# Attention and feed-forward on one core: load order of the first keys and queries, warm-up products, and the order of the first scores and weighted values

## Chip, cores, metric

One core of a Trainium2 chip. The metric is device time in microseconds (us) of one execution, the median over several runs of the same program. Traces give times from the start of their own span; a span is some 1.7 us shorter than the time of the run (236.55 us of 238.26 before).

## The reference, cut to what matters

```python
# q, k, v: (4, 8, 768, 64); sort_net: (4, 8, 8, 8); out: (3072, 512)
P = sort_net                       # 8 blocks of 96 rows in each head
for _ in range(5):                 # Sinkhorn: exp, then rows and columns normalized
    ...
k_sorted = einsum('bhij,bhjcd->bhicd', P, k_blocks)      # blocks mixed with P
v_sorted = einsum('bhij,bhjcd->bhicd', P, v_blocks)
attn = softmax(q_block @ k_sorted_block.T / 8)           # inside each block of 96
x = attn @ v_sorted_block
h = relu(x @ w_in)                                       # feed-forward, 512 -> 2048 -> 512
out = (s * h * h + b) @ w_out
```

## The kernel before: the parts that matter here

The work is cut into eight tiles of tokens. What concerns us is the head of the program, until the first feed-forward product (tile `hps`) of the first tile of tokens; from there on TensorE is nearly always busy (198.7 of the 201.3 us from 30.73 to 232 us). In the head, q, k and v of batch 0 are loaded (float32 in memory, bfloat16 on chip); q is transposed on TensorE; the Sinkhorn loop runs on VectorE (DVE) and ScalarE (ACT); a small product `pe` spreads its result over the partitions; from that a mixing matrix `pd1` is built; products with it sort the keys (`tk`, cast into `ks`) and the values (`tv`, cast into `vs`); then come scores (`sc`), exp (`at`), weighted values (`pv`, normalized into `x`), and transposes of `x`.

```python
psa = ... tile_pool(name="psa", bufs=3, PSUM)     # large PSUM tiles
psb = ... tile_pool(name="psb", bufs=2, PSUM)     # small ones

nc.sync.dma_start(out=s_bc, in_=moe_s.to_broadcast([128, 1]))   # one scalar to 128 partitions
nc.sync.dma_start(out=b_bc, in_=moe_b.to_broadcast([128, 1]))
...
load_q(0, slice(0, 64));  load_k(*brows(0));  load_v(*brows(0));  load_q(0, slice(64, 128))
...
def warm_up(n):                       # products of zeros that nobody reads, meant to keep the clock up
    for _ in range(n):
        wp = psb.tile([128, 256], FP, tag="b", name="wp")
        nc.tensor.matmul(out=wp, lhsT=zt[:, 0:128], rhs=zt, start=True, stop=True)

def v_piece0(d0, n, eng):             # n of the 64 columns of the sorted v
    ps = (psa if n > 8 else psb).tile([128, n, 64], FP)          # written shorter here
    for t in range(n):
        nc.tensor.matmul(out=ps[:, t, :], lhsT=vb[0:64, :, d0 + t], rhs=pd1[0:64]...)
    evac(VS[0][:, :, d0:d0 + n], ps..., eng)
...
warm_up(38)
q_half(0, "s")                        # 48 transposes of q's first half, two copies on ACT
warm_up(12)
build_pd1()                           # the product pe, then three small steps on DVE
k_piece(...) x 4                      # 48 products, 16 casts on DVE and ACT
v_piece0(0, 16, "v"); v_piece0(16, 16, "s"); v_piece0(32, 16, "v")
s_piece(0, 0); s_piece(0, 1)
v_piece0(48, 16, "v")
s_piece(0, 2); s_piece(0, 3)
q_half(1, "s")
for hp in range(NHP):
    p_piece(0, hp, 0, 2)
t_piece(0, "v", 0, 2)
s_piece(1, 0); s_piece(1, 1)
ffn1(0, ...)                          # the first feed-forward products
```

In the trace before, TensorE took q's transposes (8.34 us), the twelve warm-ups (9.21) and the product `pe` (12.46) in the order of the program: what stands ahead of `build_pd1` on TensorE also runs ahead of it.

The softmax here doesn't subtract the row's maximum and nothing guards it: scores larger than these inputs give would overflow.

Of the kernel before, what the change touches and what calls it, by code (L numbers as in the profile page):

```python
# [9 lines left out]
FP = mybir.dt.float32  # L10
# [8 lines left out]
def kernel(  # L19
# [18 lines left out]
    NHP = H // 2  # L38
# [28 lines left out]
    psb = ctx.enter_context(tc.tile_pool(name="psb", bufs=2, space=bass.MemoryType.PSUM))  # L67
# [10 lines left out]
    def load_q(b, part=slice(0, 128)):  # L78


        if b == B - 1:
            qr[b] = qrp.tile([128, TQ, H, D], BF, tag="qr", name=f"qr{b}")
            for t in range(TQ):
                nc.gpsimd.dma_start(
                    out=qr[b][:, t],
                    in_=q[b][:, t * 128:(t + 1) * 128, :].rearrange("h p d -> p h d"))
            return
        if b not in qr:
            qr[b] = qrp.tile([128, H, TQ, D], BF, tag="qr", name=f"qr{b}")
        nc.gpsimd.dma_start(  # L90
            out=qr[b][part].rearrange("p h t d -> p h (t d)"),
            in_=q[b].rearrange("h (p t) d -> p h (t d)", t=TQ)[part])

    def load_k(rows, prow, n=1):
        for c0 in range(0, BLK, BLK // n):
            cs = slice(c0, c0 + BLK // n)
            nc.gpsimd.dma_start(out=kb[prow, cs, :], in_=kraw[rows, cs, :])

    def load_v(rows, prow):
        nc.gpsimd.dma_start(out=vb[prow, 0:BLK, :], in_=vraw[rows])  # L100

    def brows(b):
        return slice(b * 64, (b + 1) * 64), slice((b % 2) * 64, (b % 2) * 64 + 64)
# [17 lines left out]
    new_vs(1)  # L121
    nc.scalar.activation(out=warm, in_=warm, func=AF.Exp)

    load_q(0, slice(0, 64))
    load_k(*brows(0))
    load_v(*brows(0))
    load_q(0, slice(64, 128))

# [47 lines left out]
    ks = const.tile([128, 64, BLK], BF)  # L176

    def warm_up(n):
        for _ in range(n):
            wp = psb.tile([128, 256], FP, tag="b", name="wp")  # L180
            nc.tensor.matmul(out=wp, lhsT=zt[:, 0:128], rhs=zt, start=True, stop=True)  # L181

    def zero_pad(r0):
# [9 lines left out]
    between = [lambda: zero_pad(BLK), lambda: zero_pad(BLK + 16), lambda: None,  # L193
               lambda: None, lambda: None]
# [45 lines left out]

    QT = {}

    def q_half(half, eng):

        if half == 0:
            QT[0] = qtp.tile([128, NHP, S], BF, tag="qt", name="qt0")
        pr = slice(half * 64, half * 64 + 64)
        ps = psa.tile([128, 2, 1024], BF, tag="a", name="tq")
        for hp in range(NHP):
            for t in range(TQ):  # L250
                c0 = (hp % 2) * TG + t * 64
                for e in range(2):
                    nc.tensor.transpose(out=ps[e * 64:(e + 1) * 64, hp // 2, c0:c0 + 64],  # L253
                                        in_=qr[0][pr, 2 * hp + e, t, :], identity=ident[pr, pr])
        for a in range(2):
            evac(QT[0][:, 2 * a:2 * a + 2, half * TG:(half + 1) * TG].rearrange(
                     "q b (p t) -> q b p t", t=TQ),
                 ps[:, a, 0:2 * TG].rearrange("q (b t p) -> q b p t", b=2, t=TQ), eng)
# [22 lines left out]
    def k_piece(b, c0, nc2, nb, eng):  # L281




        pr = brows(b)[1] if nb == 1 else slice(0, 128)
        rhs = (pd1[pr] if b < 2 else pd2[pr, b - 2]).rearrange("p e m i -> p (e m i)")
        if nc2 * nb > 8:
            ps = psa.tile([128, nc2, nb * 64], FP, tag="a", name="tk")
        else:  # L290
            ps = psb.tile([128, nc2, nb * 64], FP, tag="b", name="tk")
        for c in range(nc2):
            nc.tensor.matmul(out=ps[:, c, :],  # L293
                             lhsT=kb[pr, c0 + 2 * c:c0 + 2 * c + 2, :].rearrange("p c d -> p (c d)"),
                             rhs=rhs, start=True, stop=True)
        g0 = (b % 2) * 32

        def half(cp):
            if b == 0:
                cs = slice(c0 + cp, c0 + 2 * nc2, 2)  # L300
            else:
                cs = slice(cp * (BLK // 2) + c0 // 2, cp * (BLK // 2) + c0 // 2 + nc2)
            for e in range(2):
                evac(ks[e * 64:(e + 1) * 64, g0:g0 + nb * 32, cs].rearrange(
                         "p (b g) c -> p b g c", b=nb),
                     ps[cp * 64:(cp + 1) * 64].rearrange(
                         "p c (b e g) -> p e b g c", b=nb, e=2)[:, e], eng)

        half(0)
        return lambda: half(1)  # L310

    def v_piece0(d0, n, eng):

        if n > 8:
            ps = psa.tile([128, n, 64], FP, tag="a", name="tv")
        else:
            ps = psb.tile([128, n, 64], FP, tag="b", name="tv")
        for t in range(n):
            nc.tensor.matmul(out=ps[:, t, :], lhsT=vb[0:64, :, d0 + t],  # L319
                             rhs=pd1[0:64].rearrange("p e m i -> p (e m i)"),  # L320
                             start=True, stop=True)
        evac(VS[0][:, :, d0:d0 + n], ps[0:BLK].rearrange("p t g -> p g t"), eng)
# [42 lines left out]
    def s_piece(t, hp):  # L365

        b, half = divmod(t, 2)
        g0 = (b % 2) * 32 + hp * NB + half * HB
        sc = psa.tile([BLK, 2, 512], FP, tag="a", name="sc")
        for n in range(HB):  # L370
            for e in range(2):
                pr = slice(e * 64, (e + 1) * 64)
                q0 = (half * HB + n) * BLK
                nc.tensor.matmul(out=sc[:, e, n * BLK:(n + 1) * BLK], lhsT=ks[pr, g0 + n, :],  # L374
                                 rhs=QT[b][pr, hp, q0:q0 + BLK], start=True, stop=True)
        at = atp.tile([BLK, 2, TG], BF, tag="at", name="at")
        nc.scalar.activation(out=at, in_=sc[:, :, 0:TG], func=AF.Exp, scale=scale)  # L377
        AT[t, hp] = at

    def p_piece(t, hp, n0=0, nn=HB):  # L380

        b, half = divmod(t, 2)
        at = AT[t, hp]
        if t not in X:
            X[t] = xp.tile([BLK, HB, d_model], BF, tag="x", name="x")
        x = X[t]
        atf = at.rearrange("p e t -> p (e t)")
        if nn < HB:
            p1 = psb.tile([128, 512], FP, tag="b", name="pv")
            pv = [p1[:, e * nn * VW:(e + 1) * nn * VW] for e in range(2)]  # L390
            pvv = p1[0:BLK, 0:2 * nn * VW].rearrange("p (e n w) -> p e n w", e=2, w=VW)
        else:
            p2 = psa.tile([128, 2, 512], FP, tag="a", name="pv")
            pv = [p2[:, 0], p2[:, 1]]
            pvv = p2[0:BLK, :, 0:nn * VW].rearrange("p e (n w) -> p e n w", w=VW)
        for e in range(2):
            for n in range(n0, n0 + nn):
                c0 = (e * HB + n) * BLK
                m = 128 if c0 + 128 <= 2 * TG else BLK
                gi = e * 32 + hp * NB + half * HB + n  # L400
                nc.tensor.matmul(out=pv[e][0:m, (n - n0) * VW:(n - n0 + 1) * VW],  # L401
                                 lhsT=atf[:, c0:c0 + m],
                                 rhs=VS[b][:, gi, :], start=True, stop=True)
        rec = rtp.tile([BLK, 2, HB], FP, tag="rec", name="rec")
        nc.vector.reciprocal(out=rec[:, :, 0:nn], in_=pvv[:, :, :, D])  # L405
        nc.vector.tensor_tensor(  # L406
            out=x[:, n0:n0 + nn, hp * 128:(hp + 1) * 128].rearrange("p n (e d) -> p e n d", e=2),
            in0=pvv[:, :, :, 0:D],
            in1=rec[:, :, 0:nn].unsqueeze(3).broadcast_to([BLK, 2, nn, D]), op=ALU.mult)
# [141 lines left out]
    def build_pd1():  # L551
        pt = block_rows(0)
        nc.vector.tensor_tensor(  # L553
            out=pd1, in0=hmask.rearrange("p (m e) i -> p e m i", e=2),
            in1=bass.AP(tensor=pt.tensor, offset=pt.offset,
                        ap=[list(pt.ap[0]), [0, 2], [0, NHP], list(pt.ap[1])]),
            op=ALU.mult)
# [10 lines left out]


    warm_up(38)  # L570
    q_half(0, "s")
    warm_up(12)
    build_pd1()
    k_piece(0, 0, 16, 1, "v")()
    k_piece(0, 32, 16, 1, "s")()
    k_piece(0, 64, 8, 1, "v")()
# [2 lines left out]
    v_piece0(16, 16, "s")  # L579
    v_piece0(32, 16, "v")  # L580
    s_piece(0, 0)
    s_piece(0, 1)
    v_piece0(48, 16, "v")
    s_piece(0, 2)
    s_piece(0, 3)
    q_half(1, "s")
    for hp in range(NHP):
        p_piece(0, hp, 0, 2)
    t_piece(0, "v", 0, 2)
    s_piece(1, 0)  # L590
    s_piece(1, 1)
# [105 lines left out]
```

## Time and profile before

| | before |
|---|---|
| median of runs | 239.0 us (238.2 to 239.3) |
| PE / DVE / ACT busy | 95 / 55 / 46 % of the span |
| product `pe` starts | 12.46 us |
| v products can start (v landed) | 16.65 us |
| sorted keys complete | 19.73 us |
| sorted v complete | 25.30 us |
| first feed-forward product | 30.73 us |
| from there to the end of the span | 205.8 us |
| full clock, by the trace's clock records | 5.25 to 15.49 us, and from 32.56 us |

The first two rows are from the runs and the page, the rest from the timeline and the table of stretches. Busy time alone misleads here: in the head, PE is "busy" with warm-ups and with half-speed work. The prediction shows the lines.

### The profile page before, as it was taken

The page shows a single profiled execution, that of the slowest core. Times are in us where ns is not written, and L with a number is a line of the kernel's source. Part 1 is how long each engine was busy: PE and PEld are TensorE (multiplying, and loading weights), DVE is VectorE, ACT ScalarE, POOL GpSimd, SP SyncE. Part 2 cuts the span into 40 slices and gives each one's busy share as a digit, 9 for nine tenths or more (in the row PEclk, how much of TensorE's full clock was granted, in tenths as well). Part 3 has the DMA queues.
Part 4 walks back from the last instruction along what each step waited for, and adds up shares of the span by engine and source line. Part 5 has one row for each costly group of instructions (what it writes and reads, how often), then busy time and mean ns, then how long its engine had stood idle before and what let it go on. Part 6 is the DMA issues. An engine that isn't in the chain of part 4 may idle for free.

```text
span 236.6 us, 4840 instructions
## 1 busy us (share of the span) xinstructions
PE 223.9 (95%) x2029; PEld 134.3 (57%) x2048; DVE 129.8 (55%) x264; ACT 108.8 (46%) x157; POOL 43.7 (18%) x57
## 2 busy tenths in 40 slices
PE   8849799989999999999999999999999999999994
PEld 4548698845545555555555455656554556654443
DVE  4776557967994458866434744434352544342221
ACT  5357556435538542477775321566422225660000
POOL 7820000099960000295000000000000000000000
PEclk9985579999999999999999999999999999999999
DMA  4999999996999996499992414630024142001122
GB/s 57 192 198 212 225 192 206 218 221 121 146 156 175 257 320 124 111 100 109 122 74 90 111 47 115 87 89 1 3 87 105 56 116 42 0 0 44 59 77 89
DMA packets 38231, 28.11 MB, mean 119 GB/s; under 512 B 26433, under 2 KB 32577, under 8 KB 37697
## 3 DMA queue, kind: packets, MB, share of 16 engines
q0 software_dynamic: 13600, 15.21, 45.6%
q1 hardware_dynamic: 24464, 12.53, 22.9%
q8 instruction: 16, 0.26, 0.5%
q10 hardware_dynamic: 144, 0.07, 0.1%
q14 instruction: 7, 0.05, 0.1%
HBM read 29.63 MB, written 8.65 MB: 162 GB/s over the span
## 4 chain that ended last, share of the span: by engine, by line
PE 85%; DMA 6%; DVE 5%; issue 2%; POOL 1%; ACT 1%; POOLq 0%
PE hps L458 35%; PE ops L501 33%; DMA vb<-in_v_dram 6%; PE sc L374 3%; PE pv L401 3%; PE tv L319 2%; PE tk L293 2%; PE ops L486 1%; DVE x L406 1%; PE tq L268 1%; PE tv L349 1%; DVE gt L463 1%; DVE ks L237 1%; DVE vn L237 1%; PE tq L253 1%
## 5 line engine op out<-in xcount | busy, mean ns | idle before, releaser
L458 PE MATMUL hps<-xt,wi 128*128 128x384 bf16 (+1 forms) x576 | 88.7, 310 | 1.0 <-DVE xt L237 1.0
L501 PE MATMUL ops<-wo,gt 128*128 128x512 bf16 x349 | 84.0, 379 | 1.4 <-issue 0.5
L462 ACT ACTIVATE rt<-hps 128x768 bf16<-128x768 f32 (+1 forms) x72 | 53.3, 740 | 51.6 <-PE hps L458 50.5
L458 PEld LDWEIGHTS <-wi 128*128 128x128 bf16 x576 | 53.8, 99 | 31.1 <-issue 2.3
L463 DVE TENSOR_TENSOR gt<-rt 128x768 bf16<-128x768 bf16 (+1 forms) x72 | 42.0, 585 | 41.2 <-ACT rt L462 40.6
L501 PEld LDWEIGHTS <-gt 128*128 128x128 bf16 x368 | 33.6, 98 | 36.8 <-issue 0.6
L475 DVE SCALAR_TENSOR_TENSOR ot<-ops,s_bc,bias 128x512 f32<-128x512 f32 x23 | 17.2, 749 | 40.4 <-PE ops L501 40.3
L377 ACT ACTIVATE at<-sc 96x768 bf16<-96x768 f32 x32 | 24.2, 802 | 33.1 <-PE sc L374 33.1
L406 DVE TENSOR_TENSOR x<-pv,rec 96x512 bf16<-96x512 f32 (+1 forms) x36 | 22.6, 628 | 1.3
L239 ACT CAST ks<-tk 64x512 bf16<-64x512 f32 (+1 forms) x32 | 16.0, 501 | 7.7 <-PE tk L293 7.4
L237 DVE CAST ks<-tk 64x512 bf16<-64x512 f32 (+1 forms) x32 | 18.1, 565 | 1.3 <-PE tk L293 0.9
L622 POOL TENSOR_TENSOR csum<-csum,wo 128x512 f32<-128x512 f32 x14 | 17.6, 1256 | 1.0
L401 PEld LDWEIGHTS <-at 96*128 96x128 bf16 (+1 forms) x256 | 11.9, 104 | 4.1 <-ACT qt L239 1.0
L401 PE MATMUL pv<-vs,at 96*128 96x66 bf16 (+1 forms) x256 | 12.9, 199 | 0.8 <-DVE rec L405 0.6
L405 DVE RECIPROCAL rec<-pv 96x8 f32<-96x8 f32 (+1 forms) x36 | 6.9, 192 | 8.9 <-PE pv L401 8.8
L374 PEld LDWEIGHTS <-ks 64*96 64x96 bf16 x256 | 8.3, 132 | 5.7 <-issue 5.4
L374 PE MATMUL sc<-qt,ks 64*96 64x96 bf16 x256 | 10.7, 223 | 0.0
L181 PE MATMUL wp<-zt 128*128 128x256 bf16 x50 | 9.3, 310 | 1.1 <-DVE warm L113 1.1
L293 PEld LDWEIGHTS <-kb 64*128 64x128 bf16 x192 | 6.4, 95 | 5.4 <-issue 4.9
L293 PE MATMUL tk<-pd,kb 64*128 64x64 bf16 x192 | 7.8, 191 | 0.9 <-DVE pd L553 0.9
L239 ACT CAST vn<-tv 128x1024 bf16<-128x1024 f32 x6 | 6.1, 1012 | 4.1 <-PE tv L349 2.2
L319 PE MATMUL tv<-pd,vb 64*128 64x64 bf16 x64 | 6.0, 271 | 2.0 <-DMA vb<-in_v_dram 1.5
(71 smaller groups left out, 106.6 us busy)
## 6 DMA issues: line engine op xcount, KB each, us to landing
out_dram<-ot SPq DMA_DIRECT2D x23, 256.0 KB, 2.2
kb<-in_k_dram POOLq DMA_DIRECT2D x4, 768.0 KB, 10.4
vb<-in_v_dram POOLq DMA_DIRECT2D x4, 768.0 KB, 19.0
wi<-in_moe_w_in_dram POOLq DMA_DIRECT2D x2, 1024.0 KB, 19.1
wo<-in_moe_w_out_dram POOLq DMA_DIRECT2D x2, 1024.0 KB, 30.3
qr<-in_q_dram POOLq DMA_DIRECT2D x2, 768.0 KB, 27.7
dv<-vn SPq DMA_DIRECT2D x6, 256.0 KB, 7.0
vs<-dv POOLq DMA_DIRECT2D x4, 384.0 KB, 11.9
```

The lines of the kernel that those rows point to most:

```text
L237: nc.vector.tensor_copy(out=out, in_=in_)
L239: nc.scalar.copy(out=out, in_=in_)
L293: nc.tensor.matmul(out=ps[:, c, :], lhsT=kb[pr, c0 + 2 * c:c0 + 2 * c + 2, :].rearrange("p c d -> p (c d)"), rhs=rhs, start=True, stop=True)
L374: nc.tensor.matmul(out=sc[:, e, n * BLK:(n + 1) * BLK], lhsT=ks[pr, g0 + n, :], rhs=QT[b][pr, hp, q0:q0 + BLK], start=True, stop=True)
L377: nc.scalar.activation(out=at, in_=sc[:, :, 0:TG], func=AF.Exp, scale=scale)
L401: nc.tensor.matmul(out=pv[e][0:m, (n - n0) * VW:(n - n0 + 1) * VW], lhsT=atf[:, c0:c0 + m], rhs=VS[b][:, gi, :], start=True, stop=True)
L406: nc.vector.tensor_tensor(out=x[:, n0:n0 + nn, hp * 128:(hp + 1) * 128].rearrange("p n (e d) -> p e n d", e=2), in0=pvv[:, :, :, 0:D], in1 ...
L458: nc.tensor.matmul(out=hps[:, f, 0:nt], lhsT=wi_at(hp, f0 + f), rhs=xt_at(t, hp, n0, nn), start=(hp == 0), stop=(hp == NHP - 1))
L462: nc.scalar.activation(out=rt[:, :, 0:nt], in_=hps[:, :, 0:nt], func=AF.Relu)
L463: nc.vector.tensor_tensor(out=gt[:, f0:f0 + 2, c0:c0 + nt], in0=rt[:, :, 0:nt], in1=rt[:, :, 0:nt], op=ALU.mult)
L501: nc.tensor.matmul(out=ops, lhsT=gt[:, f, m * 128:(m + 1) * 128], rhs=wo_at(f), start=(f == 0), stop=(f == NF - 1))
L622: nc.gpsimd.tensor_tensor(out=csum, in0=csum, in1=wo_at(f), op=ALU.add)
```

## The change

Its intent: start the keys' large load first; let warm-ups run without waits between their two buffers and fill more of the wait for `pd1`, so that TensorE's clock stays up; take the last v product off the wait for the first exp by splitting it and putting its halves between scores; and use the wait of the weighted values for q's second half.

```diff
+    load_k(*brows(0))
     load_q(0, slice(0, 64))
-    load_k(*brows(0))
     load_v(*brows(0))
...
     def warm_up(n):
+        wp = psb.tile([128, 256], FP, tag="b", name="wp")
         for _ in range(n):
-            wp = psb.tile([128, 256], FP, tag="b", name="wp")
             nc.tensor.matmul(out=wp, lhsT=zt[:, 0:128], rhs=zt, start=True, stop=True)
...
-    def q_half(half, eng):
+    def q_half(half, eng, between=lambda hp: None):
...
         for hp in range(NHP):
+            between(hp)
             for t in range(TQ):
...
     warm_up(38)
     q_half(0, "s")
-    warm_up(12)
+    warm_up(20)
     build_pd1()
+    warm_up(6)
...
     s_piece(0, 0)
+    v_piece0(48, 8, "v")
     s_piece(0, 1)
-    v_piece0(48, 16, "v")
+    v_piece0(56, 8, "v")
     s_piece(0, 2)
     s_piece(0, 3)
-    q_half(1, "s")
-    for hp in range(NHP):
-        p_piece(0, hp, 0, 2)
+    q_half(1, "s", lambda hp: p_piece(0, hp, 0, 2))
```

## The prediction

Passages that gave rules or figures of the hardware that no trace of this case shows are cut, and the cuts marked. With them go the end of the 38 warm-ups ahead of q and, as a term of the sum, the time of the twenty behind it. That term, added to q's landing at 10.3 us and 0.94 us of transposes, came to 13.4 us for the start of the spreading product `pe`, "about 1 us" after the 12.46 of the kernel before. This 1.0, the other delays (2.2, 3.3, none) under **Cost** and **Sum**, and the 12.4 us of rival A hold that term, and so does the total: a gain of 1.5 us, from 239.0 to 237.5. "Warm" and "cold" mean full and half granted clock. That a dense stretch of work would hold the clock was the author's estimate, from the drop at 15.49 us after 1.96 us of work in 3.42.

> **What bounds the kernel now.** I read the page first: PE is busy 95% of 236.6 us, and the chain that ended last is 85% PE. Its part by line tells where this change can act.
>
> ```profile
> PE 85%; DMA 6%; DVE 5%; issue 2%; POOL 1%; ACT 1%; POOLq 0%
> ```
>
> The 6% DMA is one wait, for v of batch 0, and it lies before 17 us; from the first feed-forward product on, the chain is almost wholly PE. So what the head of the program (0 to 30.7 us) saves moves everything after it, and nothing after it is changed. Next I read the chain in order of time for 0 to 45 us: the head's skeleton.
>
> ```profile
> 2.67 13.99 DMA vb<-in_v_dram
> 16.65 0.14 issue
> 16.79 4.37 PE tv L319 x47
> ...
> 22.49 1.38 PE tv L319 x14
> ...
> 24.08 1.23 DVE vs L237
> ...
> 25.36 1.49 PE tq L253 x48
> ```
>
> V lands at 16.65, then v products, scores, a fourth v product that starts at 22.49 behind the first exp, its eviction until 25.3, the second half of q (25.36), and only then weighted values. Then the table by stretch of each engine's busy time and granted clock; after the clock column stand DMA share and GB/s:
>
> ```profile
> 8.66:12.07 3.41, 2.57 (x52) 1.58 (x45) 2.76 (x13) 1.74 (x4) 2.55 (x5) 1.00 0.96 198
> 12.07:15.49 3.42, 1.96 (x50) 1.82 (x50) 1.93 (x6) 0.74 (x2) 0.88 (x1) 1.00 1.01 195
> 15.49:18.90 3.41, 2.11 (x24) 2.14 (x25) 3.29 (x7) 3.33 (x7) 0.54 (x1) 0.50 1.18 210
> ...
> 29.14:32.56 3.42, 3.42 (x39) 3.01 (x40) 0.98 (x2) 1.84 (x3) 0.00 (x0) 0.50 1.07 185
> 32.56:35.97 3.41, 3.41 (x53) 3.06 (x51) 2.96 (x12) 1.85 (x5) 0.00 (x0) 1.00 1.24 207
> ```
>
> From 15.49 to 32.56 us, 17 us, TensorE ran at half clock. Last I read the timeline of the head:
>
> ```profile
> 9.21 2.02 PE L181 MATMUL wp<-zt 128*128 128x256 bf16 x12
> 12.46 0.40 PE L222 MATMUL pe<-sn,emat 32*128 32x64 f32 x2 [1.23 <-DVE sn L210]
> 13.77 1.56 PE L293 MATMUL tk<-pd,kb 64*128 64x64 bf16 x48 [0.90 <-DVE pd L553]
> 14.43 4.90 DVE L237 CAST ks<-tk 64x512 bf16<-64x512 f32 x8 [0.71 <-PE tk L293]
> 14.89 4.83 ACT L239 CAST ks<-tk 64x512 bf16<-64x512 f32 x8 [2.68 <-PE tk L293]
> 19.36 1.22 DVE L237 CAST vs<-tv 96x1024 bf16<-96x1024 f32 x1
> 30.73 1.46 PE L458 MATMUL hps<-xt,wi 128*128 128x192 bf16 x8
> ```
>
> A second limit shows here: the sorted keys' casts keep DVE and ACT full from 14.4 to 19.7, whatever the clock of TensorE. They start as soon as the mixing matrix pd is there (13.7).
>
> [...] the low stretch is 17.07 us, five windows of 3.41, and the drop follows a window (12.07 to 15.49) with only 1.96 us of PE, most of it on half the rows. [...] Warm-ups until 5.20 us took 4.06 us for 19 or 214 ns each, [...] the twelve later ones 2.02/12 = 168 ns[...]. There the wait for the other of two buffers binds, and this the change removes. [...] q, k, v land at 7.85, 12.2, 16.65 in order of issue (issue start plus time to landing).
>
> **The change part by part.**
>
> 1. *Keys first.* The bytes before v are the same. K took about 4.4 us (12.2−7.85). Q's half is 512 packets of 768 bytes, and DMA moved only 29 to 33 GB/s at 3 to 4 us and reached 181 to 198 at 5 to 6: about 1 us is lost to that start. If the keys' large packets meet less of it, or hide it, v lands up to 1 us earlier (estimate: 15.7 to 16.6). K lands near 8 and q not before 9.4; with q's own 2 us of packets (its other half) and 0.4 to landing I take 10.3, range 9.3 to 11.5, against 7.85.
>
> 2. *Warm-ups in one buffer.* The order listing of the two programs shows the PE waits in them gone. [...] But q is now late[...]. After them stand 20 warm-ups[...]. The product that spreads the Sinkhorn result [...] is in order behind q and the warm-ups, although its input is ready at 12.3. **Cost: about 1 us** on pd, the casts and all behind them; 2.2 if q lands at 11.5, 3.3 or more if the clock drops in the idle time. None if q lands at 9.3.
>
> 3. *Six more warm-ups*[...] lie in the 0.9 us that PE waits for pd: free, and with the twenty they make the window before k and v dense, so the drop at 15.49 should not come then. V products ran cold at 4.19/47 = 89 ns; warm I estimate half. K's products were warm already.
>
> 4. *Fourth v product in two halves, in the other pool, between scores.* It no longer waits for the exp. With pd d later than now, DVE ends its casts at 19.3+d, first v eviction 20.6+d, third 21.8+d, the halves 0.62 each: v complete at 23.2+d if PE is warm. If PE is cold: scores from 20.95 at 16 x 40 ns = 0.64, half a v product 8 x 0.09 = 0.72, again 0.64, 0.72: the last half ends at 23.7, evicted by 24.5, plus d. Now: 25.3.
>
> 5. *Q's second half between weighted values.* Now 1.49 us of transposes lie before the first weighted value (26.77). Afterwards they fill PE while DVE works its four 0.6 us pairs. From v complete to the first feed-forward product it took 30.73−25.3 = 5.4; without the block and with its wait I get about 4.0 warm, 4.9 cold.
>
> **Sum**, start of the feed-forward. Warm: 23.2+1.0+4.0 = 28.2, a gain of 2.5, plus some 0.8 for the first 1.8 us of the feed-forward that ran at half clock: 3.3 us. Cold from about 19 or 22 us: 24.5+1.0+4.9 = 30.4, a gain of 0.3; q landing at 9.3 adds 1. Clock dropped before the twenty warm-ups (d = 3.3, warm afterwards): 30.5, a gain of 0.2, or a loss of 1 us if it then drops again. Weights 0.45, 0.3 and 0.25, and an even chance of the earlier q in the first two: about 1.9 us. I take off a little because the stretch is full of waits that I don't see, and because the sparse v and score stage (DVE-bound) may itself drop the clock: **1.5 us**, from a middle of the runs before of 239.0 to **237.5 us**.
>
> **The rivals.**
>
> A. *A wait takes the place of the one removed*: q late, spreading product behind it, pd 2 to 3 us later. For: strict order on PE, the idle time grows to a whole clock window. Against: the start of the loads may shrink, and 20 warm-ups plus q at 9.3 would end just at 12.4, where the result is ready. Makes 238.5 to 240.
>
> B. *DVE and ACT are the bound*: the casts of 4.9 us and the evictions of v follow pd whatever the clock, so a warm TensorE buys little and only parts 4 and 5 count. For: DVE is full from 14.4 to 20.6. Against: DVE then idles 0.7 and 1.6 us waiting for cold PE. Makes about 238.
>
> C. *The clock holds throughout*: the whole sum, with v earlier and q at 9.3: 4 to 4.5 us, so 234.5 to 235. For: the dense 26 warm-ups. Against: from 16 to 24 us PE then works under half of the time, on half its rows, like the window that dropped it.
>
> **Range and chances.** The runs before spread by 1.1 us (238.2 to 239.3)[...]; the cases span 234.5 to 240. Predicted 237.5, 8 in 10 within 235.6 to 239.6. Two per cent is 4.8 us: faster needs the best case of everything, 0.06; slower needs the loss of a whole clock period on top of A, 0.02.
>
> **What would show it.** Part 1: landings of k near 8, q near 10.3, v before 16.6. Part 2: PE idle before the first transposes, the spreading product at about 13.4, key casts starting near 15.4. Part 3: granted clock 1.0 beyond 15.5 us. Part 4: last v eviction near 24. Part 5: transposes between weighted values, first feed-forward product between 28 and 30, and from there to the end the same length as now (206 us). I am wrong if q lands past 11.5, if the clock drops before 13 us, or if the tail after the feed-forward's start shrinks or grows by more than 1 us.

## The result, and the profile after

The changed kernel took 241.81 us (median of four runs, 241.45 to 242.63) against 239.0 us. A ratio here is the mean time of one kernel's fast runs over that of the other's of the same rounds, so not quite the ratio of the medians that are quoted: it is 1.0128, with a 95% interval of 1.009 to 1.0166. Executions over 1.5% slower than the fastest of the same kernel are left out of the means. The change makes the kernel 1.3% slower: still "within 2%", but above the range of 235.6 to 239.6.

The page follows the chain of waits and work that ended last back from the last instruction. Its split by engine, for the changed kernel:

```profile
PE 88%; DMA 4%; DVE 4%; ACT 2%; issue 1%; POOL 0%; DVEq 0%; POOLq 0%
```

The DMA share fell from 6% to 4%, but it is another transfer. The chain in order of time (start, length, what) shows which, and what follows it:

```profile
1.98 10.47 DMA qr<-in_q_dram
...
12.50 1.49 PE tq L254 x24
13.98 4.03 PE wp L181 x20
18.02 0.37 PE pe L222 x2
...
19.28 1.10 PE tk L294 x32
```

V has left the chain. In its place stand q, landing at 12.45 us, its transposes, and then 4.03 us of warm-ups, products that nobody reads, on the path to the product `pe`. The timeline of the same stretch (start, length, engine, line, instruction, count; in brackets the idle time before and what ended it):

```profile
1.13 5.64 PE L181 MATMUL wp<-zt 128*128 128x256 bf16 x38 [1.13 <-DVE warm L113]
11.59 0.21 DVE L210 TENSOR_TENSOR sn<-sn,rrec 32x64 f32<-32x64 f32 x1
12.50 1.49 PE L254 MATMUL tq<-ident,qr 64*64 64x64 bf16 x48 [5.73 <-DMA qr<-in_q_dram]
13.92 4.10 PE L181 MATMUL wp<-zt 128*128 128x256 bf16 x20
17.95 0.43 PE L222 MATMUL pe<-sn,emat 32*128 32x64 f32 x2
19.28 1.56 PE L294 MATMUL tk<-pd,kb 64*128 64x64 bf16 x48
34.25 1.46 PE L459 MATMUL hps<-xt,wi 128*128 128x192 bf16 x8
```

The Sinkhorn loop is done at 11.8 us (11.59 + 0.21). Its result then waits 6.1 us for TensorE, which sat idle for 5.7 us until q came and afterwards ran warm-ups. The table of stretches (busy time of PE, PEld, DVE, ACT and POOL, then the granted clock as a share of the full one, DMA share, GB/s), cut at the clock's own steps, tells why twenty warm-ups took 4.1 us:

```profile
7.28:10.70 3.42, 0.00 (x0) 0.00 (x0) 2.72 (x14) 0.51 (x2) 3.42 (x6) 1.00 0.80 101
10.70:14.11 3.41, 1.61 (x50) 1.49 (x51) 0.97 (x5) 0.08 (x1) 1.37 (x2) 0.50 1.13 227
14.11:17.52 3.41, 3.41 (x18) 2.43 (x16) 0.00 (x0) 1.42 (x2) 0.54 (x1) 0.50 1.13 190
17.52:20.94 3.42, 3.28 (x63) 2.75 (x62) 1.66 (x5) 0.53 (x1) 0.00 (x0) 1.00 1.12 209
```

A whole window without a product, then half clock for two windows: warm-ups at 4.03/20 = 202 ns, against 2.36/20 = 118 at full clock in the later run with the scalars behind q.

Put side by side, from the two traces:

| us | before | after | difference |
|---|---|---|---|
| q's first half landed | 7.8 | 12.45 | +4.6 |
| product `pe` starts | 12.46 | 17.95 | +5.5 |
| sorted keys complete | 19.73 | 25.21 | +5.5 |
| sorted v complete | 25.30 | 29.27 | +4.0 |
| first feed-forward product | 30.73 | 34.25 | +3.5 |
| end of the span | 236.55 | 240.90 | +4.35 |

So 5.5 us are lost up to `pe`, 2.0 come back between there and the feed-forward, and 0.8 are lost again after it. The profiled pair overstates the end: its "after" (242.63 us) is the slowest run of four, its "before" (238.26 us) close to the fastest. By medians the difference is 2.8 us.

### The profile page after: what moved, and what is told of

Same layout as the page of the kernel before. It is cut to its first block, busy times and chain, and to the rows that moved or that the text cites. A ratio compares the mean times of both kernels' runs of the same rounds, so it can differ in the third digit from the quotient of the medians.

```text
span 240.9 us, 4888 instructions
## 1 busy us (share of the span) xinstructions
PE 228.1 (95%) x2062; PEld 138.7 (58%) x2062; DVE 129.6 (54%) x265; ACT 108.9 (45%) x157; POOL 43.7 (18%) x57
## 4 chain that ended last, share of the span: by engine, by line
PE 88%; DMA 4%; DVE 4%; ACT 2%; issue 1%; POOL 0%; DVEq 0%; POOLq 0%
PE hps L459 34%; PE ops L502 34%; DMA qr<-in_q_dram 4%; PE pv L402 4%; PE sc L375 4%; PE tk L294 3%; PE tv L320 2%; PE wp L181 2%; PE ops L487 1%; PE tq L254 1%; PE tq L269 1%; ACT ks L239 1%; PE tv L350 1%; DVE gt L464 1%; DVE x L407 1%; DVE vn L237 1%
## 5 line engine op out<-in xcount | busy, mean ns | idle before, releaser
L502 PE MATMUL ops<-wo,gt 128*128 128x512 bf16 x368 | 86.9, 380 | 0.0
L459 PEld LDWEIGHTS <-wi 128*128 128x128 bf16 x576 | 54.5, 100 | 31.2 <-issue 2.3
L181 PE MATMUL wp<-zt 128*128 128x256 bf16 x64 | 10.6, 340 | 1.1 <-DVE warm L113 1.1
L181 PEld LDWEIGHTS <-zt 128*128 128x128 bf16 x64 | 7.5, 122 | 3.5 <-DVE warm L113 1.1
L254 PE MATMUL tq<-ident,qr 64*64 64x64 bf16 x96 | 3.6, 240 | 5.7 <-DMA qr<-in_q_dram 5.7
## 6 DMA issues: line engine op xcount, KB each, us to landing
vs<-dv POOLq DMA_DIRECT2D x4, 384.0 KB, 11.8
```

The costliest lines, as they stand in the source:

```text
L459: nc.tensor.matmul(out=hps[:, f, 0:nt], lhsT=wi_at(hp, f0 + f), rhs=xt_at(t, hp, n0, nn), start=(hp == 0), stop=(hp == NHP - 1))
L502: nc.tensor.matmul(out=ops, lhsT=gt[:, f, m * 128:(m + 1) * 128], rhs=wo_at(f), start=(f == 0), stop=(f == NF - 1))
```

## The experiments

Theory after the comparison: the load order alone does the harm, by way of late q, a clock that drops while TensorE waits, and warm-ups in order ahead of `pe`; the other parts gain. The main rival: the new order of work does the harm. The kernel before, run beside each batch, had medians of 238.81, 238.81 and 238.83 us.

**Load order undone.** The changed kernel with

```diff
-    load_k(*brows(0))
     load_q(0, slice(0, 64))
+    load_k(*brows(0))
```

> The changed kernel with the first half of q loaded before the keys again, all else as changed. Theory (late q, with twenty warm-ups and the spreading product in order behind it, costs the time): q lands near 7.9 us instead of 12.45, the spreading product waits for the Sinkhorn result only and starts at 12.3 to 12.6 instead of 17.95, key casts start near 14.4, and the first feed-forward product comes 1.5 to 3 us before the 30.7 of the kernel before; time 236 to 238 us, so faster than the kernel before (239.0) by 1 to 3 us and than the changed one (241.8) by 4 to 6. Rival (the split fourth v product, or the transposes between weighted values, cost the time): stays at 241 to 242 us.

Measured: 237.57 us, ratio to before 0.9961 (0.9926 to 0.9996). Product `pe` at 12.46 us, key casts from 14.43, first feed-forward product at 28.74. The theory holds; the new order of work gains 2.0 us in the head. But the time fell by 1.2 only, which the later section on the clock takes up. Swapping two lines costs the changed kernel 4.2 us (241.81 − 237.57).

**Load order alone.** The kernel before with the two loads swapped, nothing else.

> The kernel before with only the two loads swapped. Theory: q lands near 12.4 us, its transposes and the twelve old warm-ups follow, TensorE was idle from 8.4 to 12.4 and drops to half clock for some of it; spreading product at 15.9 to 16.6 instead of 12.46, first feed-forward product some 3.5 to 4.5 us later than 30.7; time 242 to 244 us, slower than the changed kernel because it has not parts 4 and 5. Rival (load order is harmless, the warm-ups in one buffer or the new order of work cost the time): 238.5 to 239.5 us.

Measured: 243.94 us, ratio 1.0221 (1.0186 to 1.0256). Q's transposes at 12.46 us, `pe` at 16.55, first feed-forward product at 35.67. The time and `pe` came as the theory said; the first feed-forward product was 4.9 us later than before the change, more than the 3.5 to 4.5 expected. The rest of the change makes up 2.1 us of it (243.94 − 241.81).

**Why is q so late? Scalar loads out of the way.** Both traces have two more transfers at the start: the broadcasts of the scalars `s` and `b`, 128 packets of 4 bytes each, on another queue. The view of DMA queues of the changed kernel (queue, packets, MB, share of 16 engines), first for 4 to 7 us, while the keys' packets of 12 KB run in q0 and the scalars wait in q1:

```profile
q0 software_dynamic: 43, 0.53, 93.8%
q1 hardware_dynamic: 43, 0.00, 1.1%
```

And for 7.5 to 10 us, when q's packets of 768 bytes run:

```profile
q0 software_dynamic: 249, 0.19, 60.8%
q1 hardware_dynamic: 205, 0.00, 8.5%
```

One scalar packet for each packet of keys, 43 and 43; so most of the scalars were left over when q's turn came, and then there are nearly as many of them as of q's. (The ratio isn't fixed: in the kernel before, from 4 to 6 us, 406 packets of q ran beside 38 of the other queue.) Data moves slowly meanwhile: the table of stretches has 38 GB/s at 7.5 to 8.5 us and 85 at 8.5 to 9.5. Two runs test whether the scalars delay q. First the two scalar loads moved far behind the first loads (some 59 us later, as it turned out):

```diff
-    nc.sync.dma_start(out=s_bc, ...); nc.sync.dma_start(out=b_bc, ...)
...
     v_read(1, nc.sync)
+    nc.sync.dma_start(out=s_bc, ...); nc.sync.dma_start(out=b_bc, ...)
```

> The changed kernel with the two broadcast loads of the scalars s and b (128 packets of 4 bytes each) issued some 45 us later. Theory of why q lands at 12.45 and not at the 10.3 that I estimated: those small packets [...] were left over behind the keys' large packets and then slow q's small ones. Without them q lands at 9.5 to 10.7 us, and the spreading product comes at 12.8 to 16; time 239 to 241 us. Rival (q's packets are slow by themselves, or its descriptors come late): q lands at 12 to 12.6 us as before, time 241.3 to 242.3.

The head did as expected: q's transposes started at 10.38 us. The time is no result: the profiled run took 240.04 us, three others 247.7 to 250.8, flagged slow. In the profile the scalar `s`, issued at 60.1 us, landed 11.2 us later, shortly before its first use; whether it came later still in the slow runs I can't say, since they have no trace. So I repeated it in another way: the two loads put into the queue of the large loads, behind q's second half (`nc.gpsimd.dma_start` after `load_q(0, slice(64, 128))`).

> The changed kernel with the two scalar broadcasts put into the queue of the loads, behind the second half of q, so that they are neither in front of the first loads nor late. (In the run with the scalars loaded 45 us later the head was as the theory said, q at 10.4 us, but three of four times were 8 to 11 us longer, so that edit brought a trouble of its own and must be repeated in another way.) Theory: q lands at 10.2 to 10.6 us, spreading product at 14.5 to 15.3 (twenty warm-ups behind q, partly at half clock), first feed-forward product near 31, time 239 to 240.3 us in all runs. Rival (something else than those packets made q late): q at 12 us or later, 241.3 to 242.5 us.

Measured: 240.14 us (238.24 to 241.09), ratio 1.0053 (1.0002 to 1.0105). The timeline of TensorE in its profiled run:

```profile
10.28 0.95 PE L254 MATMUL tq<-ident,qr 64*64 64x64 bf16 x48 [2.35 <-DMA qr<-in_q_dram]
11.16 2.36 PE L181 MATMUL wp<-zt 128*128 128x256 bf16 x20
13.45 0.43 PE L222 MATMUL pe<-sn,emat 32*128 32x64 f32 x2
```

Q comes 2.2 us earlier (10.28 against 12.50) by moving 1 KB out of its way, and this is the 10.3 of the prediction. Here the clock held through the shorter wait, the twenty warm-ups took 2.36 us, and `pe` started at 13.45, not at the 14.5 to 15.3 expected (the feed-forward at 29.67, not near 31).

That the clock held is partly luck. With the scalars late, q came as early (10.38 us), yet the clock dropped at 11.88, the warm-ups took 3.87 us and `pe` started at 15.06. In every trace the clock's steps lie 3.41 us or a multiple of it apart, but they start at another moment in each run (5.25, 15.49 and 32.56 us before; 10.70, 17.52, 24.35 and 38.00 in the changed kernel). The profiled run was the fastest of the four, 238.24 us; the others, without a trace, took 240.1 to 241.1, so that two of the four lie outside the 239 to 240.3 expected. Their mean granted clock was 0.961 to 0.964 against 0.971: an estimated 3.3 us or more of additional half clock (0.007 x 237 / 0.5), which would fit a drop in this wait.

**The wait filled.** 85 warm-ups ahead of q's transposes in place of 38, and none behind them; q still late.

> The changed kernel with 85 warm-ups ahead of q's transposes and none of the twenty behind them. Theory (half of the 5.5 us by which the spreading product is late is not q itself but the clock that drops in the idle time, and the twenty warm-ups that then run cold in front of it): TensorE has no idle stretch over 1 us before q, the clock stays full until 16 us at least, the spreading product starts at 13.3 to 14.2 us, the first feed-forward product at 29 to 31; time 238 to 239.7 us. Rival (q's landing alone sets it, the warm-ups behind it are hidden): within 0.7 us of the changed kernel, 241 to 242.5.

Measured: 238.16 us (237.27 to 239.13), ratio 0.9996 (0.9946 to 1.0045).

```profile
12.39 0.94 PE L254 MATMUL tq<-ident,qr 64*64 64x64 bf16 x48 [0.19 <-DMA qr<-in_q_dram]
13.26 0.43 PE L222 MATMUL pe<-sn,emat 32*128 32x64 f32 x2
```

With q at the same late time, `pe` is only 0.8 us later than before the change. The other 4.7 of the 5.5 us are not q itself.

**Nothing behind q.** The line `warm_up(20)` taken out, the 38 ahead left as they are, so that the clock still drops.

> The changed kernel without the twenty warm-ups between q's transposes and the spreading product; q still late. Theory (of the 5.5 us by which the spreading product came late, 4.0 are these twenty at half clock in front of it and only 1.5 is q's own): TensorE idles until q lands at 12.4 us, the clock drops in between, transposes take 1.5 us, the spreading product starts at 13.9 to 14.2, keys at half clock, first feed-forward product at 30 to 31.5, time 238.3 to 240, so 2 to 3.5 us faster than the changed kernel. Rival (the half clock and q's landing cost the time, the warm-ups only fill a wait): 241 to 243 us.

Measured: 239.7 us, ratio 1.0038 (1.0015 to 1.006). The timeline of TensorE:

```profile
13.89 0.68 PE L222 MATMUL pe<-sn,emat 32*128 32x64 f32 x2
14.51 1.46 PE L181 MATMUL wp<-zt 128*128 128x256 bf16 x6
```

`pe` started at 13.89 us, as expected; the first feed-forward product at 31.58, just past the 30 to 31.5 expected. From `pe` to the first cast of the keys it took 3.1 us instead of the changed kernel's 2.0, all of it at half clock: `pe` itself is slower (0.68 us against 0.43), the keys' products too (2.74 us for 48 against 1.56), and the six warm-ups behind `pe` end at 15.97 us, after the mixing matrix (15.42), so that here part 3 is not free. Taking out twenty products whose results nobody reads saves 2.1 us. So the 5.5 us are: q's landing 0.8, the twenty warm-ups behind it 17.95 − 13.89 = 4.1, and the rest, 0.6, mostly the slower transposes (1.49 against 0.94 us).

**Does v's landing bind?** Old load order, rest as changed, scalars behind q's second half, so that all of the first loads come earlier.

> The old load order, all else as changed, with the scalar broadcasts behind the second half of q. v should land at about 15 us, 1.5 us before the 16.45 of the run with the old load order alone. Theory (v's landing is not what binds: the casts of the sorted keys, which start when the mixing matrix is there at 13.7 us, keep DVE and ACT until 19.7): scores start at 20.6 to 20.9 us as without it and the time stays within 0.7 us of that run's 237.6. Rival (the wait for v on the chain is a real bound): scores start over 1 us earlier and the time falls to 236.3 or less.

Measured: 237.04 us (median of the three fast runs), ratio 0.9935 (0.9904 to 0.9967); the fourth run, 241.23 us, was slow. V landed at 14.8 us (issue at 2.7 plus 12.1), 1.9 earlier than before the change; scores started at 20.81 us against 20.82 with the old load order alone, and the first feed-forward product at 28.64 against 28.74. The wait for v, 6% of the chain before, is worth nothing: the casts of the keys on DVE and ACT end at 19.7 us either way.

**Warm-ups alone.** The kernel before with one buffer for each group of warm-ups, 20 in place of 12, and 6 more.

> The kernel before with only the warm-ups changed: one buffer for each group, 20 in place of 12 and 6 more. With q early they lie in idle time. Theory (the gain of the old-load-order run comes from the split fourth v product and the transposes between weighted values, not from the warm-ups): spreading product at 12.4 to 12.6 us, key products at 13.8, first feed-forward product at 30.2 to 30.8, time 238 to 239.3, the same as before. Rival (a clock held longer is what gained): clock full beyond 19 us and the time 237 to 237.8.

Measured: 238.33 us, ratio 0.9987 (0.9958 to 1.0016): the same. In its trace the clock was full until 18.40 us instead of 15.49, and the first feed-forward product came at 30.47. Three more us at full clock bought nothing that can be told from zero. (`pe` started at 11.94 us, earlier than the 12.4 to 12.6 expected, because the Sinkhorn loop ended 0.5 us earlier in that run.)

**The split v product alone,** and **q's transposes between weighted values alone,** each put into the kernel before.

> The kernel before with only the fourth v product split in two halves between the scores. Theory: v complete near 23.9 us instead of 25.3, q's second half (1.5 us of transposes) still ahead of the weighted values, first feed-forward product at 29.3 to 30 instead of 30.73; a part of it lost again to the clock, time 237.9 to 238.7. Rival (parts 4 and 5 give nothing apart, only together): 238.6 to 239.2.

> The kernel before with only the transposes of q's second half put between the weighted values. Theory: v is complete at 25.3 us as before, weighted values start at once instead of 26.77, but q's second half comes later; first feed-forward product at 29.7 to 30.3, time 238 to 238.9. Rival: within 0.3 us of the kernel before.

The split: 237.24 us, ratio 0.9932 (0.99 to 0.9965). V complete at 23.74 us instead of 25.30, first feed-forward product at 28.99 instead of 30.73, all a little better than expected. `pe` came 0.5 us earlier in that run, but the keys' casts ended at 19.74 us as before, so the gain lies behind them. The timeline of DVE in its head ends v like this, against one cast at 24.08 before:

```profile
21.03 1.82 DVE L237 CAST vs<-tv 96x1024 bf16<-96x1024 f32 x2 [0.80 <-PE tv L319]
23.05 0.69 DVE L237 CAST vs<-tv 96x512 bf16<-96x512 f32 x1 [0.20 <-PE tv L319]
```

The transposes between: 238.41 us, ratio 0.9974 (0.9945 to 1.0003), not clear of zero. From v complete to the first feed-forward product it took 4.98 us (25.59 to 30.57) instead of 5.43, so a gain of 0.45 exists in the trace; but in that run the keys' products ran at half clock (2.71 us), their casts and thus v ended 0.3 to 0.5 us later than before, the first feed-forward product came at 30.57 us, past the 29.7 to 30.3 expected, and the clock rose later.

**Fillers.** The old load order, rest as changed, with 48 more warm-up products written into the tiles of v products and weighted values before those are computed, to hold the clock through the head:

```diff
-    v_piece0(0, 16, "v"); v_piece0(16, 16, "s"); v_piece0(32, 16, "v")
+    v_piece0(0, 16, "v", 20); v_piece0(16, 16, "s", 8); v_piece0(32, 16, "v", 4)
...                    # and 4 ahead of each half of the fourth, 2 ahead of each weighted value
```

> The old load order, all else as changed, with 48 more warm-up products in the places where TensorE waits: 20, 8 and 4 ahead of the first three v products, 4 ahead of each half of the fourth, 2 ahead of each of four weighted values. Theory (half of what the shorter head saves is lost again because the first 4.6 us of the feed-forward run at half clock; over six runs the time from its first product to the end is 205.0 us plus 0.45 of the time until the clock is full): clock full from about 6 us to the end, first feed-forward product at 27 to 28.5 us, then 205 us to the end of the span, time 233.5 to 235.5, faster than both kernels. Rival (sparse small products [...] drop the clock all the same, or the fillers delay real work): drop before 26 us, first feed-forward product at 28.5 to 30, time 237 to 239.

It failed: 242.52 us (median of three fast runs; a fourth, 245.59 us, was slow), ratio 1.0099 (1.0012 to 1.0186), outside the rival's 237 to 239 us too. The fillers delayed real work already at full clock: the second cast of v, on ACT, started at 21.46 us against 19.75 with the old load order alone. Then the clock dropped at 23.01 us all the same, further fillers ran at half clock ahead of real work, and the first feed-forward product came at 35.14. In one run, 239.36 us, the mean granted clock was 0.999, so it hardly dropped, and the run was still slower than all seven of the kernel before. The trace gave one thing more. Here v products ran at full clock; the row of 19.8 to 21.35 us in the table of stretches:

```profile
19.80:21.35 1.55, 1.55 (x17) 1.50 (x16) 0.42 (x1) 0.00 (x0) 0.00 (x0) 1.00 1.13 211
```

Sixteen weight loads in 1.50 us are 94 ns each, as long as before the change at half clock (4.19/47 = 89 ns). The view of the tile says the same for the changed kernel, whose first sixteen v products ran at full clock, and then for the kernel before at half clock (minimum, median, maximum in ns):

```profile
L320 PEld LDWEIGHTS <-vb x17: 163/206/220, 20.6 to 22.0; 64*128 64x128 bf16 x17
```

```profile
L319 PEld LDWEIGHTS <-vb x48: 163/208/240, 16.8 to 20.9; 64*128 64x128 bf16 x48
```

V's weights are read with a step of 64 elements; keys' products, whose weights lie together, took 1.56/48 = 33 ns at full clock. That the step is the reason is argued, since no run changed it; that the clock isn't is measured.

**Where half of a shorter head goes.** Over all thirteen traces, the time from the first feed-forward product to the end is not constant: 205.7 to 207.1 us. It follows how long the clock stayed low after that product. In three of them:

| | first product | clock full from | low for | to the end |
|---|---|---|---|---|
| warm-ups alone | 30.47 | 32.06 | 1.59 | 205.70 |
| changed kernel | 34.25 | 38.00 | 3.75 | 206.65 |
| old load order | 28.74 | 33.35 | 4.61 | 207.06 |

A straight line through all thirteen, 205.01 + 0.45 x low time, leaves at most 0.18 us. I read the slope as what half speed costs, and so a head that ends early, while the clock is still low, gives nearly half of its gain back (0.45 us of each us that then runs slow). With the old load order the feed-forward starts 2.0 us earlier than before the change, but 4.6 instead of 1.8 us of it run slow: 1.2 lost again. The spread of one kernel's runs goes with the clock as well: of the 21 runs of the kernel before beside the batches, the seven with a mean granted clock of 0.964 took 237.57 to 238.53 us, the fourteen with 0.955 to 0.957 took 238.76 to 239.44.

What raises or drops the clock the runs do not isolate. With TensorE occupied for 3.24 to 3.42 us of each of the stretches of 3.41 us from 16.28 to 26.52 us (the run with the old load order), mostly with small products on half the rows, the clock stayed at half; and in the profiled run with fillers it dropped at 23.01 us after a stretch in which the profile, which models the ends of products, has TensorE occupied throughout (19.60 to 23.01 us, 3.41 of 3.41).

## Why the prediction was wrong, point by point

The steps are named as in the prediction.

- **Part 1, keys first: this step failed first.** It took q's landing as 10.3 us, range 9.3 to 11.5; it was 12.45 (and k 8.8 instead of near 8). I saw the slow start of the loads (29 to 33 GB/s at 3 to 4 us) and took it for a cost of starting. A good part of it was the scalars' packets: with the old order and the scalars behind, the rate at 3 to 4 us was 52 to 75 GB/s, and q landed at 6.4 us instead of 7.8. Putting the keys first did not take these packets out of q's way; most of them were left for q, and cost it 2.2 us. Without them its transposes started at 10.28. That v would land up to 1 us earlier was right (16.1 against 16.65), and worthless: v didn't bind.
- **Part 2, warm-ups: the order on TensorE was right, the size of the loss was not.** "In order behind q and the warm-ups" is what happened (q's transposes at 12.50 us, warm-ups at 13.92, `pe` at 17.95), and "3.3 or more if the clock drops in the idle time" is the case that came, with 5.5. The waits between the two buffers did go: at full clock twenty warm-ups took 2.36 us, 118 ns each, against 168 before. But against the predicted 13.4 us `pe` was 4.5 late, and the terms that were too small are q's landing, by 2.2, the transposes at half clock, by 0.5 (1.49 us against 0.94), and, with the rest of 1.8, the twenty warm-ups, which took 4.03 us at half clock. The idle stretch became 5.7 us and held a whole window of 3.41 us without work, after which the clock dropped. I gave the dropped clock a weight of 0.25. Of the five traces with keys first and 38 warm-ups ahead of q, four dropped before `pe` (the changed kernel, load order alone, nothing behind q, scalars late); only the one with the scalars behind q held.
- **Part 3, six more warm-ups: free, as said** (0.83 us at full clock: in the changed kernel they end at 19.14 us, the mixing matrix at 19.23), but of no use: a clock held longer gained nothing measurable. And "warm I estimate half" for the v products was wrong: 89 ns at half clock, 94 at full. The estimate took the clock for their bound; the weight loads, busy for 1.50 of 1.55 us at full clock, fit better.
- **Part 4, the split: right, and the whole gain within the noise.** 1.56 us for v in the trace (predicted 24.5 at half clock, 23.2 at full; 23.74 measured alone), 1.6 us in the time.
- **Part 5, between weighted values: right at the size given for half clock** (4.9 predicted; 4.98 measured, alone, with the old load order and in the changed kernel). In the time it could not be told from zero.
- **The sum** had its third case, "d = 3.3, warm afterwards", at a gain of 0.2 us in the head. With d, the delay of the mixing matrix, at 5.5 in place of 3.3 the same sum gives a loss of 2.0; cold from 24.35 us on, it lost 3.5.
- **Rival A** is what happened, "makes 238.5 to 240": the right story, two us short. **Rival B**, DVE and ACT as the bound, was right too, and the run with v early shows it: scores at 20.81 us with v there at 14.8, against 20.82 with the old load order alone. The keys' casts took DVE 4.90 us in the kernel before, where the clock fell to half among them, and 4.95 in the changed one, at full clock until 24.35 of the 24.89 us at which they end.
- The stated signs of error both came: q past 11.5 us, and a clock drop before 13. The third didn't: the tail grew by 0.8, under the 1 us allowed, but I had not seen that it depends on the clock.

Three versions beat both kernels with an interval clear of 1: the kernel before with the split alone (237.24 us), the changed kernel with the old load order (237.57), and the same with the scalars moved (237.04). All are under 1% faster than the kernel before, and their intervals overlap.

## What to carry to other kernels

Before moving a load forward, look at what shares the DMA engines at that moment and at what stands in program order behind the load that moves back: the harm here was a kilobyte of scalars ahead of q (2.2 us), and idle-filling products behind it that had become part of the path (4.1 us). Fill a wait with work ahead of the instruction that waits, never between it and the work that others depend on (85 warm-ups ahead of q: 238.16 us; 38 ahead and twenty behind: 241.81). A wait at the head of the chain is only worth removing if nothing else ends at the same time; here two casting engines did, at 19.7 us.
